# Seven block products for every second down product in a Fourier mixing and SoLU kernel

## The chip, the core and the metric

The kernel runs on one core of a Trainium2 chip, in FP32. The metric is the device time of one execution in microseconds, the median of several runs. The core has TensorE (PE in the profile; its weight loads are PEld), VectorE (DVE), ScalarE (ACT), GpSimd (POOL) and SyncE (SP, which here only issues transfers). Each works through its own instructions in the order of the program, and semaphores make one wait for another.

## The reference, cut to what matters

```python
def _attn_ref(x):                        # x: 8 x 3136 x 256
    X = np.fft.fft(x, axis=1)
    X = np.fft.fft(X, axis=2)
    return X.real.astype(np.float32)

def _moe_ref(x, w_in, w_out, g_ln):      # 25088 x 256, 256 x 1024, 1024 x 256
    h = x @ w_in
    h_max = np.max(h, axis=-1, keepdims=True)
    e = np.exp(h - h_max)
    sm = e / (np.sum(e, axis=-1, keepdims=True) + 1e-09)
    solu = h * sm
    mu = np.mean(solu, axis=-1, keepdims=True)
    var = np.mean((solu - mu) ** 2, axis=-1, keepdims=True)
    ln = (solu - mu) / np.sqrt(var + 1e-06) * g_ln
    return ln @ w_out
```

The output of the first function, as 25088 rows, is the input of the second.

## The kernel before

The Fourier transform over the 3136 positions is split as 49 x 64. The part over 49 is the "first transform" of a pair of batches, the part over 64 the "second transform"; the transform over the 256 features is folded into `w_in`. `g_ln` and the mean are folded into `w_out` (`Wo`), so that what is left after the down product is one scale for each row, `rs`.

A **unit** is one index of the 49-part of one pair of batches: 128 rows of an even part `q[:, 0:128]` and an odd part `q[:, 128:256]`. Even plus and minus odd give two sets of 128 rows, its two *signs*; a unit with index 0 has one sign only. There are 4 pairs of 25 units, 100 in all. Units run as a pipeline of **steps**: step i brings in unit i and does the down product of unit i - 4. Of each unit:

```python
    def up(t, c):                                   # half c of the up product, on TensorE
        ps = ps_h.tile([P, FF], FP32, tag=f"h{c}", name=f"ps_h{c}")
        for half in range(2):
            fs = slice(half * HW, (half + 1) * HW)
            nc.tensor.matmul(ps[:, fs], t.q[:, c * P : (c + 1) * P], Wi[:, c, fs], start=True, stop=True)
        return ps

    # even(t, ps): VectorE, t.ev = w_mid * t.r + ps
    # transform1(pr, s): first transform of a later pair: TensorE into ps_m, ScalarE copies it to z
    # transform2(pr, k1): second transform: TensorE into ps_m; take2(t, ps): ScalarE copies it to t.q
    # spread(t): a small transfer of one row of t.q to t.r

    def join(t, ps):                                # VectorE
        t.nmax = small.tile([P, 2], FP32, tag="nmax", name="nmax")
        for s in t.signs:
            t.h[s] = fpool.tile([P, FF], FP32, tag="h", name="h", bufs=2)
            nc.vector.tensor_tensor_reduce(out=t.h[s], in0=t.h[0] if s else t.ev, in1=ps, ...)

    def expo(t):                                    # ScalarE
        ...
        for s in t.signs:
            nc.scalar.mul(out=t.neg[:, s : s + 1], in_=t.nmax[:, s : s + 1], mul=-1.0)
            t.u[s] = fpool.tile([P, FF], FP32, tag="u", name="u", bufs=2)
            nc.scalar.activation(out=t.u[s], in_=t.h[s], func=ACT.Exp, bias=t.neg[:, s : s + 1],
                                 accum_out=t.esum[:, s : s + 1])

    # product(t, s): VectorE, u = h * u with its sum;  square(t, s): ScalarE, sum of (usum - FF * u)^2

    def stats(t):                                   # GpSimd
        nc.gpsimd.tensor_scalar(out=es[:, n], in0=t.esum[:, n], scalar1=1e-9, scalar2=1e-3, ...)
        nc.gpsimd.tensor_tensor(out=es2[:, n], in0=es[:, n], in1=es[:, n], op=ALU.mult)
        nc.gpsimd.tensor_scalar(out=v[:, n], in0=t.ssq[:, n], scalar1=float(FF) ** -3, ...)
        nc.gpsimd.tensor_tensor(out=v[:, n], in0=v[:, n], in1=es2[:, n], op=ALU.add)
        nc.gpsimd.tensor_tensor(out=t.rs[:, n], in0=v[:, n], in1=neg_half[:, n], op=ALU.pow)

    def turn_blocks(t, s):                          # VectorE: transposes u in 32 x 32 blocks, to v
        ...
    def move_blocks(batch, units, ...):             # 16 transfers put the blocks of two units into uT
        ...
    def down(t, s):                                 # TensorE
        uT = t.batch.uT[:, t.w].rearrange("p c i (n s) -> p c (i n) s", s=2)
        ps = ps_m.tile([P, D], FP32, tag="m", name="ps_o")
        for c in range(KF):                         # KF = 8
            nc.tensor.matmul(ps, uT[:, c, :, s], Wo[:, c, :], start=(c == 0), stop=(c == KF - 1))
        return ps

    # scale(t, s, ps): ScalarE, ot = ps * rs;  store(t): transfers of ot to the output
```

[...] `ps_h0` and `ps_h1` take two each, `ps_m` takes four in turn (`bufs=4`). A step is, cut to the steady part:

```python
            store(units[i - lag - 1])
            begin(i)                     # even(cur, up(cur, 0)); cur.odd = up(cur, 1);
                                         # then transform2, take2 and spread of unit i + 2
            join(cur, cur.odd)
            expo(cur)
            ahead_pe(ahd, cur.k1)        # first transform of the next pair, in some steps
            ps_o = [down(old, s) for s in order]
            for s in cur.signs:
                product(cur, s)
            for s in cur.signs:
                square(cur, s)
                turn_blocks(cur, s)
            scale(old, order[0], ps_o[0])
            move_blocks(batches[-1], slice(0, 2))       # every second step
            stats(cur)
            ahead(ahd, cur.k1)           # loads, mirror sums and folds for the next pair
            scale(old, order[1], ps_o[1])
```

The first four units are turned by TensorE (`turn_whole`), before this loop is in its steady state.

## Time and profile before

| | before |
|---|---|
| time, median of 3 runs | 1189.88 us (1187.1 to 1191.42) |
| span of the profiled run | 1189.0 us |
| granted TensorE clock | 1.00 |
| TensorE / weight loads busy | 1152.6 / 874.5 us |
| VectorE / ScalarE / GpSimd busy | 912.3 / 679.9 / 505.9 us |
| first 100 us / 100 to 1145 us / rest: TensorE busy | 67.66 / 1045.00 / 39.95 us |
| moved by transfers | 185.37 MB, mean 156 GB/s |

An engine's busy time is the union of its instructions. A mean is that of one record; records of TensorE overlap, so that what a pass takes of a stream is read from start to start. The idle time of an engine is put down to what ended it. The last chain is followed back from the end of the span: each step goes to what released the instruction, or to the one before it on its engine.

### The profile page before, as it was taken

Reading aid. Unit: us, or ns where it says so; the run is one execution under the profiler, and the core shown is the slowest. Engines: PE = TensorE matmul, PEld = TensorE weight load, DVE = VectorE, ACT = ScalarE, POOL = GpSimd, SP = SyncE. Lnnn points to the kernel's source line nnn. Section 1 sums busy time; section 2 is a strip of 40 time slices with the busy share of each in tenths; the row PEclk is TensorE's granted clock in tenths of the full one; section 3 lists DMA queues with packets and bytes.
Section 4 is the critical chain, followed back from the end, with each engine's and each line's share of the span. In section 5 each row is a group of like instructions: output and inputs, shape, how many; then the busy total and the mean of one; then the engine's idle time right before and its main releaser. Section 6 shows DMA issues by size and latency. Waiting matters only on the chain.

```text
span 1189.0 us, 15738 instructions
## 1 busy us (share of the span) xinstructions
PE 1152.6 (97%) x4720; PEld 874.5 (74%) x4720; DVE 912.3 (77%) x1234; ACT 679.9 (57%) x1404; POOL 505.9 (43%) x766
## 2 busy tenths in 40 slices
PE   2989999999999999999999999999999999999998
PEld 1556777778777777777777777777777777777787
DVE  6879777777768877787778978777786887877780
ACT  3566665656546656565556656565564665655561
POOL 3025556444544444442644554443553333333323
PEclk9999999999999999999999999999999999999999
DMA  9671989958996766655996887775897464554544
GB/s 231 199 188 27 191 187 193 196 138 165 176 168 165 178 168 167 164 137 140 175 176 170 176 170 166 160 165 133 152 187 142 108 154 97 137 122 116 135 104 117
DMA packets 458452, 185.37 MB, mean 156 GB/s; under 512 B 425750, under 2 KB 440350, under 8 KB 458368
## 3 DMA queue, kind: packets, MB, share of 16 engines
q1 hardware_dynamic: 444608, 146.22, 58.3%
q0 software_dynamic: 13760, 38.16, 12.9%
q8 instruction: 38, 0.62, 0.2%
q14 instruction: 46, 0.38, 0.1%
HBM read 44.78 MB, written 38.80 MB: 70 GB/s over the span
## 4 chain that ended last, share of the span: by engine, by line
PE 93%; DMA 3%; DVE 2%; SPq 1%; issue 1%; POOL 1%; ACT 0%; DVEq 0%; ACTq 0%; POOLq 0%
PE ps_o L325 56%; PE ps_h L227 28%; PE ps L171 5%; PE ps L199 4%; DMA raw_in<-in_moe_w_in_dram 2%; PE wps L456 1%; DMA r<-q 1%; SPq L179 1%; DVE h L241 0%; POOL uT L319 0%; DMA out_dram<-ot,idx 0%; DVE y L123 0%; SPq L442 0%; PE ps_t L305 0%; DVE xa L131 0%
## 5 line engine op out<-in xcount | busy, mean ns | idle before, releaser
L325 PE MATMUL ps_o<-Wo,uT 128*128 128x256 f32 x3136 | 693.4, 379 | 1.3 <-ACT uT L310 0.9
L325 PEld LDWEIGHTS ps_o<-Wo,uT 128*128 128x128 f32 x3136 | 610.8, 196 | 64.0 <-ACT uT L310 1.1
L227 PE MATMUL ps_h<-Wi,q 128*128 128x512 f32 x800 | 360.5, 593 | 5.1 <-DVE ev L233 3.0
L272 POOL TENSOR_SCALAR es<-esum 128x2 f32<-128x2 f32 (+1 forms) x100 | 116.4, 1164 | 425.3 <-ACT u L251 425.1
L258 DVE SCALAR_TENSOR_TENSOR u<-h,u 128x1024 f32<-128x1024 f32 x196 | 239.9, 1225 | 33.5 <-ACT u L251 20.7
L227 PEld LDWEIGHTS ps_h<-Wi,q 128*128 128x128 f32 x800 | 151.5, 190 | 154.3 <-issue 142.3
L265 ACT ACTIVATE h<-u,usum 128x1024 f32<-128x1024 f32 x196 | 224.5, 1147 | 14.8 <-DVE u L258 9.0
L233 DVE SCALAR_TENSOR_TENSOR ev<-w_mid,r,ps_h 128x1024 f32<-128x1024 f32 x100 | 127.8, 1278 | 135.0 <-PE ps_h L227 127.1
L251 ACT ACTIVATE u<-h,neg 128x1024 f32<-128x1024 f32 x196 | 225.6, 1151 | 6.4
L293 DVE STREAM_TRANSPOSE v<-u 128x1024 f32<-128x1024 f32 x192 | 227.5, 1224 | 0.1
L205 ACT COPY q<-ps 128x256 f32<-128x256 f32 x100 | 37.1, 372 | 306.7 <-PE ps L199 279.5
L241 DVE CUSTOM_DVE_ANT_0 h<-ev,ps_h 128x1024 f32<-128x1024 f32 x100 | 122.1, 1221 | 48.9 <-PE ps_h L227 45.3
L330 ACT ACTIVATE ot<-ps_o,rs 128x256 f32<-128x256 f32 x196 | 90.6, 465 | 75.3 <-PE ps_o L325 66.3
L241 DVE CUSTOM_DVE_ANT_0 h<-h,ps_h 128x1024 f32<-128x1024 f32 x96 | 117.3, 1222 | 14.2 <-ACT neg L249 0.5
L337 POOL DMA_INDIRECT out_dram<-ot,idx x96 | 103.1, 1074 | 41.9 <-issue 21.4
L171 PE MATMUL ps<-y,F 98*100 98x258 f32 (+3 forms) x288 | 72.5, 389 | 25.2 <-DVE y L124 25.2
L199 PEld LDWEIGHTS ps<-T,g 128*128 128x128 f32 x400 | 60.2, 191 | 47.4 <-issue 46.9
L249 ACT ACTIVATE neg<-nmax 128x1 f32<-128x1 f32 x196 | 38.8, 198 | 71.0 <-DVE nmax L241 70.9
L280 POOL TENSOR_TENSOR rs<-v,neg_half 128x2 f32<-128x2 f32 (+1 forms) x100 | 71.7, 717 | 7.8
L171 PEld LDWEIGHTS ps<-y,F 98*100 98x100 f32 x288 | 46.3, 179 | 37.6 <-DVE y L124 24.3
L277 POOL TENSOR_SCALAR v<-ssq 128x2 f32<-128x2 f32 (+1 forms) x100 | 22.9, 229 | 117.7 <-ACT h L265 117.6
L199 PE MATMUL ps<-T,g 128*128 128x128 f32 x400 | 60.6, 274 | 0.0
(72 smaller groups left out, 493.9 us busy)
## 6 DMA issues: line engine op xcount, KB each, us to landing
uT<-v SPq DMA_DIRECT2D x752, 128.0 KB
out_dram<-ot SPq DMA_DIRECT2D x100, 128.0 KB
g<-zd POOLq DMA_DIRECT2D x72, 160.0 KB, 5.5
xa<-in_x_dram SPq DMA_DIRECT2D x28, 392.0 KB
zd<-z SPq DMA_DIRECT2D x24, 400.0 KB
raw_in<-in_moe_w_in_dram SPq DMA_DIRECT2D x4, 512.0 KB
raw_out<-in_moe_w_out_dram SPq DMA_DIRECT2D x2, 1024.0 KB
r<-q SPq DMA_DIRECT2D x100, 0.5 KB
```

The costliest lines, as they stand in the source:

```text
L171: nc.tensor.matmul(o[..., cs], F[:, 2 * t + h, :], i[..., cs], start=first, stop=True, skip_group_check=True)
L199: nc.tensor.matmul(o, g[:, k, h * P : (h + 1) * P], table, start=(h == 0), stop=True, skip_group_check=True)
L227: nc.tensor.matmul(ps[:, fs], t.q[:, c * P : (c + 1) * P], Wi[:, c, fs], start=True, stop=True)
L233: nc.vector.scalar_tensor_tensor(out=t.ev, in0=w_mid, scalar=t.r, in1=ps, op0=ALU.mult, op1=ALU.add)
L241: nc.vector.tensor_tensor_reduce(out=t.h[s], in0=t.h[0] if s else t.ev, in1=ps, scale=1.0 if s else -0.5, scalar=-3.0e38, op0=ALU.add, op1 ...
L251: nc.scalar.activation(out=t.u[s], in_=t.h[s], func=ACT.Exp, bias=t.neg[:, s : s + 1], accum_out=t.esum[:, s : s + 1])
L258: nc.vector.scalar_tensor_tensor(out=t.u[s], in0=t.h[s], scalar=1.0, in1=t.u[s], op0=ALU.mult, op1=ALU.mult, accum_out=t.usum[:, s : s + 1])
L265: nc.scalar.activation(out=t.h[s], in_=t.u[s], func=ACT.Square, bias=t.usum[:, s : s + 1], scale=-float(FF), accum_out=t.ssq[:, s : s + 1])
L272: nc.gpsimd.tensor_scalar(out=es[:, n], in0=t.esum[:, n], scalar1=1e-9, scalar2=1e-3, op0=ALU.add, op1=ALU.mult)
L293: nc.vector.transpose(out=t.batch.v[:, t.w, :, o], in_=t.u[s])
L325: nc.tensor.matmul(ps, uT[:, c, :, s], Wo[:, c, :], start=(c == 0), stop=(c == KF - 1))
L337: dma = nc.gpsimd.indirect_dma_start(out=out, out_offset=bass.IndirectOffsetOnAxis(ap=idx[:, i : i + 1], axis=0), in_=t.ot[s], in_offset=None)
```

## The change

A down product of a unit with two signs is a product of 256 rows (two signs of 128) by 1024 by 256. Cut each operand into 2 x 2 blocks: rows by sign (A1x, A2x), the inner 1024 into two halves of four chunks, the 256 columns into two of 128. The plain way needs eight block products. Strassen's scheme (in Winograd's form) needs seven, of sums of blocks. The change does this for every second unit, to take one eighth of the down product off TensorE there. The sums of weight blocks are made once (`Ws`). The sums of blocks of u (`S`, and one in place in A21) are made for each such unit on GpSimd, one step before their use. The seven products share three PSUM banks, by accumulating on top of copies, and spread over two steps: six in one, P4 in the next. To free GpSimd for the sums, the variance goes to ScalarE; only the power stays.

```diff
-    gpool = ctx.enter_context(tc.tile_pool(name="gpool", bufs=6))
+    gpool = ctx.enter_context(tc.tile_pool(name="gpool", bufs=3))
...
-    ps_m = ctx.enter_context(tc.tile_pool(name="ps_m", bufs=4, space=PSUM))
+    spool = ctx.enter_context(tc.tile_pool(name="spool", bufs=2))
+    ps_m = ctx.enter_context(tc.tile_pool(name="ps_m", bufs=1, space=PSUM))
...
+    def result(i):
+        return ps_m.tile([P, 2 * D], FP32, tag=f"m{i % 4}", name="ps_m")
...                                      (both transforms of the steady part now use result(0))
-        es = small.tile([P, 2], FP32, tag="es", name="es")
-        nc.gpsimd.tensor_scalar(out=es[:, n], in0=t.esum[:, n], scalar1=1e-9, scalar2=1e-3, ...)
...                                      (and the next three GpSimd operations)
+        nc.scalar.activation(out=es2[:, n], in_=t.esum[:, n], func=ACT.Square, bias=limits[:, 3:4], scale=1e-3)
+        for s in t.signs:
+            nc.scalar.activation(out=v[:, s : s + 1], in_=t.ssq[:, s : s + 1], func=ACT.Identity, bias=es2[:, s : s + 1],
+                                 scale=float(FF) ** -3)
...
+    def sums(t):
+        A11, A12, A21, A22 = blocks(t)
+        t.S = spool.tile([P, 3, KF // 2, P], FP32, tag="S", name="S")
+        for o, a, b, op in ((t.S[:, 0], A21, A22, ALU.add), (t.S[:, 1], t.S[:, 0], A11, ALU.subtract),
+                            (A21, A11, A21, ALU.subtract), (t.S[:, 2], A12, t.S[:, 1], ALU.subtract)):
+            nc.gpsimd.tensor_tensor(out=o, in0=a, in1=b, op=op)
+
+    def product7(o, a, b, start=False):
+        n = KF // 2
+        for c in range(n):
+            nc.tensor.matmul(o, a[:, c], b[:, c], start=start and c == 0, stop=c == n - 1, skip_group_check=True)
...
+            banks.extend(result(j) for j in (2, 3, 1))
...
+            self.C11, self.C21, self.P53 = (bank(i)[:, 0:P] for i in range(3))
...
+        def p1(self):
+            product7(self.C11, self.A11, Wo[:, 0 : KF // 2, 0:P], True)
+            nc.scalar.copy(self.C21, self.C11)
+        def p5(self):
+            product7(self.P53, self.t.S[:, 0], Ws[:, 0], True)
+            nc.scalar.copy(self.E5, self.P53)
+        def p6(self):
+            product7(self.C21, self.t.S[:, 1], Ws[:, 1])
+            nc.scalar.copy(self.X, self.C21)
+        def p2(self):
+            product7(self.C11, self.A12, Wo[:, KF // 2 :, 0:P])
+            self.scale(0, 0, self.C11)
+        def p7_p3(self):
+            product7(self.C21, self.S3, Ws[:, 2])
+            product7(self.P53, self.t.S[:, 2], Wo[:, KF // 2 :, P:])
+        def sum22(self):
+            nc.vector.tensor_tensor(out=self.C22, in0=self.C21, in1=self.E5, op=ALU.add)
+        def sum12(self):
+            nc.vector.tensor_tensor(out=self.C12, in0=self.P53, in1=self.X, op=ALU.add)
+        def p4(self):
+            product7(self.C21, self.A22, Ws[:, 3])
+            self.scale(0, 1, self.C12)
+            self.scale(1, 1, self.C22)
+            self.scale(1, 0, self.C21)
...
     def down(t, s):
-        ps = ps_m.tile([P, D], FP32, tag="m", name="ps_o")
+        ps = bank(2 * s)[:, 0:D]
```

The loop is written anew from step 5 on. `by_seven(i)` holds for odd units with two signs, but for the last unit. In an odd step `seven` is set, in an even step it is not:

```python
            for s in prv.signs:                  # the unit of the step before
                square(prv, s)
            stats(prv)
            if by_seven(i - lag + 1):
                sums(units[i - lag + 1])
            ps = up(cur, 0)
            if half:
                half.p4(); half = None
            for t, s, ps_o in rest:
                scale(t, s, ps_o)
            rest = []
            if seven:
                half = Down(old, ...); half.p1()
            else:
                ps_o = down(old, order[0])
            other_pairs(i, ahead_pe)             # first transform, in some steps
            even(cur, ps)
            if seven:
                half.p5()
            store(units[i - lag - 1])
            cur.odd = up(cur, 1)
            join(cur, 0)
            if seven:
                half.p6()
            elif len(order) == 2:
                rest.append((old, order[1], down(old, order[1])))
            expo(cur, 0)
            if seven:
                half.p2()
            else:
                scale(old, order[0], ps_o)
            second_transform(i + 2)              # transform2, take2, spread
            join(cur, 1)
            expo(cur, 1)
            if seven:
                half.p7_p3()
            product(cur, 0)
            if seven:
                half.sum22()
            product(cur, 1)
            if seven:
                half.sum12()
            for s in cur.signs:
                turn_blocks(cur, s)
            if cur.w:
                move_blocks(batches[-1], slice(0, 2))
            ...                                  # transfers of the transforms
            other_pairs(i, ahead)
```

(In this listing the tests for the ends of the loop are cut.) The opening puts some of its work areas into `Ws` and `spool`, and `gpool` loads (`turn`) are issued at five chosen steps of a pair.

## The prediction

> **What bounds the kernel now.** I read the page from the top: busy shares, the chain that ended last, the costliest groups, and then the timeline of one steady step. First the busy line of the page, and its chain by engine and by line:

> ```profile
> PE 1152.6 (97%) x4720; PEld 874.5 (74%) x4720; DVE 912.3 (77%) x1234; ACT 679.9 (57%) x1404; POOL 505.9 (43%) x766
> PE 93%; DMA 3%; DVE 2%; SPq 1%; issue 1%; POOL 1%; ACT 0%; DVEq 0%; ACTq 0%; POOLq 0%
> ```

> TensorE is busy 97% of the span and is 93% of the chain. No other engine holds it up in the steady part. The groups that the change touches:

> ```profile
> L325 PE MATMUL ps_o<-Wo,uT 128*128 128x256 f32 x3136 | 693.4, 379 | 1.3 <-ACT uT L310 0.9
> L325 PEld LDWEIGHTS ps_o<-Wo,uT 128*128 128x128 f32 x3136 | 610.8, 196 | 64.0 <-ACT uT L310 1.1
> L272 POOL TENSOR_SCALAR es<-esum 128x2 f32<-128x2 f32 (+1 forms) x100 | 116.4, 1164 | 425.3 <-ACT u L251 425.1
> L330 ACT ACTIVATE ot<-ps_o,rs 128x256 f32<-128x256 f32 x196 | 90.6, 465 | 75.3 <-PE ps_o L325 66.3
> ```

> The down product (L325) is the largest group, 693 us. It has 3136 records for 196 products of eight chunks, so each FP32 matmul is two passes. A mean duration is no price here, since passes overlap. Prices come from start to start, in the timeline of one step (start, duration, engine, line):

> ```profile
> 1006.71 3.60 PE L227 MATMUL ps_h<-Wi,q 128*128 128x512 f32 x8
> ...
> 1010.15 0.61 PE L199 MATMUL ps<-T,g 128*128 128x128 f32 x4
> 1010.15 0.41 PEld L199 LDWEIGHTS ps<-T,g 128*128 128x128 f32 x3 [0.24 <-issue]
> 1010.44 1.22 DVE L241 CUSTOM_DVE_ANT_0 h<-ev,ps_h 128x1024 f32<-128x1024 f32 x1 [0.53 <-PE ps_h L227]
> ...
> 1010.59 7.08 PE L325 MATMUL ps_o<-Wo,uT 128*128 128x256 f32 x32
> 1010.79 0.37 ACT L205 COPY q<-ps 128x256 f32<-128x256 f32 x1 [3.40 <-PE ps L199]
> ...
> 1013.09 0.19 ACT L249 ACTIVATE neg<-nmax 128x1 f32<-128x1 f32 x1
> ...
> 1014.59 1.23 DVE L258 SCALAR_TENSOR_TENSOR u<-h,u 128x1024 f32<-128x1024 f32 x1
> 1014.65 1.21 POOL L272 TENSOR_SCALAR es<-esum 128x2 f32<-128x2 f32 x1 [5.33 <-ACT u L251]
> ...
> 1015.86 1.15 ACT L265 ACTIVATE h<-u,usum 128x1024 f32<-128x1024 f32 x1
> ...
> 1017.00 0.45 ACT L330 ACTIVATE ot<-ps_o,rs 128x256 f32<-128x256 f32 x1
> ...
> 1017.51 1.02 PE L227 MATMUL ps_h<-Wi,q 128*128 128x512 f32 x2
> ```

> Eight up passes take 1010.15 - 1006.71 = 3.44 us (1.72 for each of the two halves), four passes of the second transform 0.44 us, 32 down passes 6.92 us (0.216 each). A step is 10.80 us, all TensorE. In steps that also do part of the next pair's first transform, four more passes come in:

> ```profile
> 701.07 1.03 PE L171 MATMUL ps<-y,F 98*100 98x258 f32 x4
> 701.93 7.07 PE L325 MATMUL ps_o<-Wo,uT 128*128 128x256 f32 x32
> ```

> They add 0.86 us. Two plain steps are 21.6 us, two with the transform 23.3.

> [...] Here the four 128-column passes, each with its own load, come every 0.110 us, half of the 0.216 of 256 columns; the three loads in 0.41 us keep that pace too. [...] ScalarE runs both squares (1014.49 and 1015.86) before the scale at 1017.00, as in the program. [...] in the kernel before they cost almost nothing (0.5 us in total of TensorE waiting for scales). [...] the two-column es operation takes 1.21 us (median; 0.19 at the least), beginning and ending with the VectorE product at 1014.59.

> **The change part by part.** *Block products.* Seven products of four chunks, two passes each, are 56 passes of 128 columns: 56 x 0.110 = 6.16 us in place of 6.92. That removes 0.75 us from a unit, 47 units: 35 us, if TensorE never waits.

> *GpSimd.* It loses four small operations a unit (about 1.8 us, mostly lock wait) and gains four sums of 512 elements every second step; from the GpSimd row of xa<-xa,xb (2341 ns for 1020 elements) I estimate 1.17 us each, 4.7 together. They are issued a step before their use and lie beside other work.

> *VectorE* gains two 128-column sums, [...] every second step. It would need some 20 us of two steps: below TensorE.

> *ScalarE* gains three copies of 128 columns, four quarter scales for two whole ones (0.3 us each, estimated between the 0.20 of 128x1 and the 0.37 of 128x256), and three tiny operations for the variance (0.23 us each by the row of neg and its gap). It stays near 16 us of two steps. So no engine's total becomes the bound. What counts is the order.

> *The order.* Call U the moment when the second up half of an even step ends on TensorE. The code then puts the whole second-sign down product (16 passes, 3.46 us) ahead of the second transform, and ScalarE's copy of that transform (take2) ahead of the second exponential. After that ScalarE does both squares, the variance, and only then the scale of that down product (list `rest`). This scale frees the bank that the product P5 of the odd step overwrites. Along this chain, in us after U: transform data at 3.46 + 0.44 + 0.20 = 4.10 (0.20: 1010.59 to 1010.79); take2 ends 4.47; the second product starts 1.50 after the neg (1013.09 to 1014.59): 6.0; its square 1.27 later (to 1015.86): 7.27; the variance at +1.14: 8.4; three operations: 9.1; the scale ends at 9.56; P5 starts about 9.75. TensorE has only up (1.72), P1 (0.88) and perhaps a transform (0.86) to do after 3.9: it arrives at 6.5, or 7.4. It waits about 3.2 us, or 2.3. Then P5 (0.88) and the second up half (1.72): T = U + 12.35.

> From T to the next U I find no wait: P6, P2, transform, P7, P3, up, P4, down, up are 0.88 + 0.88 + 0.44 + 1.76 + 1.72 + 0.88 + 3.46 + 1.72 = 11.7 us, plus 0.86. P4 needs sum22, which VectorE has at about T + 4.7, and TensorE arrives at T + 5.7.

> So two steps take 12.35 + 11.7 = 24.1 us in place of 21.6 (+2.5), or 24.9 in place of 23.3 (+1.6). There are 45 such pairs of steps (48 odd steps from 5 to 99, less two whose finished unit has one sign, less the first), about half with transforms: 23 x 2.5 + 22 x 1.6 = 93 us. The opening and the drain I take as unchanged within 3 us. 1189.9 + 93 = 1283; with a little for locks and wake-ups, **1285 us**.

> **The rivals.** *The saving arrives.* If the scale of `rest` is in fact not late, TensorE stays the bound and 35 us come off: about 1155 us. For it: 97% busy TensorE and idle shares elsewhere. Against it: queues in program order and one bank for both products. *Weight loads become the bound.* At 0.19 us a load (record length) in series, 56 loads are 10.9 us for 6.9: +4 us a unit, about 1375 us. Against it: three loads in 0.41 us. The loads of L325 read every second element and their records are 196 ns for 190, so a spacing of 0.115 instead of 0.110 is possible; that would be 13 us in all. *GpSimd's sums hold VectorE back* (lock of up to 1.2 us on a product in the chain): +1 us in a pair, 1285 becomes 1330 at worst. *Late transfers.* P4 keeps the transposed buffer a step longer, so the 16 block moves start later. In this trace a move takes some 0.9 us of its queue; 16 are 14 us, done some 4 us ahead of need in a 24 us period. Hidden, I think.

> **Range and chances.** The chain is made of measured pieces, but has ten hand-overs; 0.1 us on each pair's whole is 4.5 us. A missed release or overlap could halve the wait (about 1235); locks could bring 1310. I take 1225 to 1315 for eight in ten. The chance that the chain does not hold at all and the saving shows is 0.10 for over 2% faster; 0.08 for within 2%; 0.82 for slower.

> **What would show it.** In the profile after: TensorE idle some 110 to 150 us more, in 45 waits of two to three us, put down to ScalarE's ot scale (or what stands ahead of it) just before the P5 passes; its busy share near 87% (1152.6 - 35 of 1285). Passes of the seven products 0.110 us apart. Two steps of 24 to 25 us in the timeline. VectorE and ScalarE shares below 80% and 65%. Wrong would be: TensorE still at 97% and pairs of steps near 20.8 us (the first rival), spacing near 0.19 (the second), waits of TensorE for sums or moves (the others).

## The result and the profile after

The changed kernel takes 1403.5 us (median of 4 runs, 1397.4 to 1407.5) against 1190.0 us: ratio 1.1793, 95% interval 1.1744 to 1.1842. The direction was predicted, the size was not: 213 us instead of 95, far outside the range.

The page of the kernel after, first the busy line, the granted TensorE clock by slices, the chain by engine, then two groups:

```profile
PE 1230.4 (88%) x5850; PEld 934.1 (67%) x5850; DVE 971.3 (69%) x1329; ACT 788.2 (56%) x1935; POOL 586.5 (42%) x558
...
PEclk9999999999899999989999999999989999899898
...
issue 45%; POOL 23%; PE 11%; DMA 6%; SPq 5%; DVE 4%; ACT 4%; POOLq 0%; DVEq 0%; ACTq 0%
...
L238 PE MATMUL ps_h<-Wi,q 128*128 128x512 f32 x800 | 421.2, 654 | 1.9 <-DVE nmax L252 1.6
...
L268 DVE SCALAR_TENSOR_TENSOR u<-h,u 128x1024 f32<-128x1024 f32 x196 | 267.8, 1368 | 93.0 <-ACT u L261 92.7
```

TensorE's share fell to 88%, but its busy time rose by 78 us although passes were taken away. The up product, which the change doesn't touch, has a mean of 654 ns where it had 593, and VectorE's product 1368 where it had 1225 (the same two groups on the page of the kernel before):

```profile
L227 PE MATMUL ps_h<-Wi,q 128*128 128x512 f32 x800 | 360.5, 593 | 5.1 <-DVE ev L233 3.0
L258 DVE SCALAR_TENSOR_TENSOR u<-h,u 128x1024 f32<-128x1024 f32 x196 | 239.9, 1225 | 33.5 <-ACT u L251 20.7
```

The mean granted clock is 0.933 where it was 1.000. So there are waits, and work beside them that became slower. The view of waits has, of TensorE's own:

```profile
PE ps_m L355 <- ACT ot L426: 94.5, 35, 5.5
...
PE ps_m L182 <- DVE y L128: 28.1, 9, 3.4
```

The first is the predicted wait: block products (L355) for ScalarE's scale of the second-sign down product (L426), 35 times where 45 were predicted. The second, of the first transform for a fold on VectorE, was not predicted. One plain pair of steps in the timeline (start, duration, engine, line):

```profile
1164.62 0.61 PE L210 MATMUL ps_m<-T,g 128*128 128x128 f32 x4
...
1166.78 1.10 PE L355 MATMUL ps_m<-Wo,uT 128*128 128x128 f32 x8
...
1170.16 0.45 ACT L426 ACTIVATE ot<-ps_m,rs 128x256 f32<-128x256 f32 x1
...
1170.76 2.05 PE L355 MATMUL ps_m<-Ws,S 128*128 128x128 f32 x8 [2.88 <-ACT ot L426]
...
1172.60 3.62 PE L238 MATMUL ps_h<-Wi,q 128*128 128x512 f32 x4
...
1176.01 1.43 PE L355 MATMUL ps_m<-Ws,S 128*128 128x128 f32 x8
```

P5 starts 0.15 us after the scale ended. Eight passes that took 0.89 us elsewhere take 1.84 (to 1172.60), and four up passes 3.41 instead of 1.72. The stretches of the same pair (us, busy time of each engine and count, then granted clock, DMA share, GB/s) say why:

```profile
1166.78:1170.76 3.98, 1.10 (x10) 0.94 (x8) 3.71 (x5) 3.78 (x11) 0.41 (x1) 0.90 0.84 177
1170.76:1172.60 1.84, 1.84 (x9) 1.84 (x9) 0.97 (x1) 0.02 (x1) 1.34 (x2) 0.50 0.68 155
1172.60:1176.01 3.41, 3.41 (x5) 1.35 (x5) 0.00 (x0) 0.27 (x1) 0.00 (x0) 0.50 0.48 136
1176.01:1177.28 1.27, 1.27 (x10) 1.27 (x8) 0.93 (x1) 0.00 (x0) 0.00 (x0) 0.69 0.00 0
1177.28:1191.79 14.51, 14.51 (x79) 11.96 (x78) 10.69 (x18) 9.16 (x23) 7.18 (x7) 1.00 0.27 60
```

After the wait TensorE is granted half its clock for 5.25 us; the 0.69 of the next stretch is a mean over the change back to full. That is 0.95 + 1.69 + 0.38 = 3.0 us lost on top of the 2.9 waited. The pair takes 1191.79 - 1164.62 = 27.2 us. Not every pair loses so much. Of the 19 waits of 2.88 us, 9 have 6.83 us of half clock at their end, as this one (from 1169.96 on), and their pairs take 27.1 to 27.2 us; ten have 3.41 us, and a plain pair takes 25.6 to 25.9.

### The profile page after: what moved, and what is told of

It is laid out like the page before. It is cut to its first block, busy times and chain, and to the rows that moved or that the text cites. A ratio compares the mean times of both kernels' runs of the same rounds, so it can differ in the third digit from the quotient of the medians.

```text
span 1402.7 us, 18541 instructions
## 1 busy us (share of the span) xinstructions
PE 1230.4 (88%) x5850; PEld 934.1 (67%) x5850; DVE 971.3 (69%) x1329; ACT 788.2 (56%) x1935; POOL 586.5 (42%) x558
## 4 chain that ended last, share of the span: by engine, by line
issue 45%; POOL 23%; PE 11%; DMA 6%; SPq 5%; DVE 4%; ACT 4%; POOLq 0%; DVEq 0%; ACTq 0%
POOL S L350 9%; SPq L326 5%; POOL out_dram L433 5%; PE ps_h L238 4%; PE ps_m L355 3%; POOL xa L137 3%; PE ps_m L421 3%; DMA uT<-v 3%; POOL rs L287 2%; POOL g L198 2%; DMA room<-in_x_dram 2%; ACT h L275 2%; DVE h L252 1%; POOL xb L117 1%; DVE u L268 1%
## 5 line engine op out<-in xcount | busy, mean ns | idle before, releaser
L238 PE MATMUL ps_h<-Wi,q 128*128 128x512 f32 x800 | 421.2, 654 | 1.9 <-DVE nmax L252 1.6
L421 PE MATMUL ps_m<-Wo,uT 128*128 128x256 f32 x1632 | 371.0, 381 | 5.1 <-ACT ot L426 2.9
L421 PEld LDWEIGHTS ps_m<-Wo,uT 128*128 128x128 f32 x1632 | 317.1, 197 | 59.2 <-issue 23.0
L268 DVE SCALAR_TENSOR_TENSOR u<-h,u 128x1024 f32<-128x1024 f32 x196 | 267.8, 1368 | 93.0 <-ACT u L261 92.7
L261 ACT ACTIVATE u<-h,neg 128x1024 f32<-128x1024 f32 x196 | 225.3, 1150 | 6.4
L355 PEld LDWEIGHTS ps_m<-Ws,S 128*128 128x128 f32 x752 | 129.4, 249 | 143.8 <-issue 137.4
L355 PE MATMUL ps_m<-Ws,S 128*128 128x128 f32 x752 | 134.0, 336 | 98.7 <-ACT ot L426 93.4
L182 PE MATMUL ps_m<-y,F 98*100 98x258 f32 (+3 forms) x288 | 83.2, 421 | 58.5 <-DVE y L128 28.1
L355 PEld LDWEIGHTS ps_m<-Wo,uT 128*128 128x128 f32 x752 | 100.4, 198 | 22.8 <-issue 20.5
L355 PEld LDWEIGHTS ps_m<-Ws,uT 128*128 128x128 f32 x752 | 99.8, 197 | 22.2 <-issue 20.8
L355 PE MATMUL ps_m<-Wo,uT 128*128 128x128 f32 x752 | 104.5, 282 | 1.1 <-ACT ot L426 1.1
L355 PE MATMUL ps_m<-Ws,uT 128*128 128x128 f32 x752 | 103.8, 281 | 0.7 <-DVE E L402 0.7
L182 PEld LDWEIGHTS ps_m<-y,F 98*100 98x100 f32 x288 | 48.0, 188 | 80.9 <-ACT ps_m L383 28.5
```

Of the source, the lines that this page charges most:

```text
L182: nc.tensor.matmul(o[..., cs], F[:, 2 * t + h, :], i[..., cs], start=first, stop=True, skip_group_check=True)
L268: nc.vector.scalar_tensor_tensor(out=t.u[s], in0=t.h[s], scalar=1.0, in1=t.u[s], op0=ALU.mult, op1=ALU.mult, accum_out=t.usum[:, s : s + 1])
L355: nc.tensor.matmul(o, a[:, c], b[:, c], start=start and c == 0, stop=c == n - 1, skip_group_check=True)
```

## The experiments

Theory A: the wait for the scale, and the half clock that follows it, make the loss. Its rivals: B, the block products are slow in themselves; C, the new loop, the buffers or the variance on ScalarE; D, a second wait, for the fold; E, GpSimd's sums shut VectorE out; F, which came up on the way, the new order of a step as such, the place of the second up half above all. Ratios are to the kernel before.

**1. The wait filled with thrown-away work** (fill).

```diff
             if seven:
+                ps = ps_h.tile([P, FF], FP32, tag="h1", name="ps_fill")
+                for half_f in (0, 1, 0):
+                    ... one half of up(cur, 1) into ps
                 half.p5()
```

> The changed kernel, with three half up products (2.58 us of passes into a bank that is free then, results thrown away) put on TensorE just before P5 in each odd step: more work, in the place where TensorE waits for the scale. Theory A (the wait of 2.9 us lets the granted clock fall to a half, and P5, the second up half and P6 then take 3 us more): the clock stays at 1.0, two plain steps take 24.2 us in place of 27.2, the whole 1290 to 1330 us. Theory B (those products are slow for a reason of their own, the block operands or GpSimd's sums): no pair of steps becomes shorter, the whole 1400 us or more.

1375.0 us, ratio 1.156 [1.154, 1.159]; clock 0.986. TensorE's timeline:

```profile
1038.67 2.74 PE L814 MATMUL ps_fill<-Wi,q 128*128 128x512 f32 x6
1041.72 1.13 PE L355 MATMUL ps_m<-Ws,S 128*128 128x128 f32 x8 [0.30 <-ACT ot L426]
1042.68 1.88 PE L238 MATMUL ps_h<-Wi,q 128*128 128x512 f32 x4
```

With 2.6 us more work in it, the plain pair is shorter: from this 1038.67 to the next at 1062.90 it is 24.2 us, not 25.6 to 27.2, and P5 and the up half have their full speed. That is theory A's pair to a tenth, and the predicted pair (24.1) too. The total missed its 1290 to 1330: in pairs with a transform TensorE waits earlier, for the fold, and there the added work only adds (they take up to 30.8 us). So D was open.

**2. Only the scale moved ahead of the squares** (scale_first), **and both moved behind P1's copy** (late_squares).

```diff
+            for t, s, ps_o in rest:
+                scale(t, s, ps_o)
+            rest = []
             if prv:
                 for s in prv.signs:
                     square(prv, s)
                 stats(prv)
```

(scale_first, the same three lines taken out below; late_squares has the squares and `stats` after `half.p1()` instead)

> The changed kernel with one move in the order of ScalarE: the scale of the even step's second down product comes before the two squares and the variance, not after them. Theory A: TensorE's wait ahead of P5 goes, a wait of about 0.6 us ahead of P6 (its copy is still behind the squares) takes its place, two plain steps take 21.5 us, the clock stays above 0.98, the whole 1185 to 1225 us. Theory B (the block products themselves are what costs): 1350 us or more.

> The changed kernel with the squares and the variance moved behind the scale and behind the copy after P1, so that neither P5 nor P6 waits for them. Theory A: a wait of about 0.7 us ahead of P4 is left (sum22 on VectorE, which now runs later); two plain steps take 21.3 to 21.8 us, the whole 1170 to 1210 us. Theory B: 1350 us or more.

1277.0 us, 1.0745 [1.0727, 1.0763], and 1282.9 us, 1.080 [1.077, 1.083]. Three moved lines are worth 126 us. Plain pairs came to 21.5 us, as A said, but the totals missed their ranges by 50 us and more. Pairs with a transform still took 23.9 to 29.6 us, with waits like this (scale_first, TensorE):

```profile
501.70 2.00 PE L182 MATMUL ps_m<-y,F 98*100 98x258 f32 x4 [3.40 <-DVE y L128]
503.49 1.91 PE L355 MATMUL ps_m<-Ws,S 128*128 128x128 f32 x8
505.19 3.34 PE L238 MATMUL ps_h<-Wi,q 128*128 128x512 f32 x4
```

The first transform waits 3.40 us for the fold of the step before, and half clock follows again (0.86 us of passes take 1.79).

**3. No seven products in the new loop** (plain).

```diff
         def by_seven(i):
-            return i % 2 and i < len(units) - 1 and len(units[i].signs) == 2
+            return False
```

> The changed kernel with no unit by seven products: the new loop, the variance on ScalarE, fewer buffers, and the old down product for every unit; all values are the reference's. Theory A (only the wait ahead of P5 and what follows from it costs): TensorE's passes cover the chain (10.8 us a step), 1188 to 1210 us. Theory C (the new order, the single bank of the two transforms or the variance on ScalarE cost most of the loss): 1280 us or more.

1235.0 us, 1.038 [1.036, 1.040]. One thing differs from what was written: the first sums, which overwrite a block of unit 1, were left in, so that unit's output isn't the reference's. Steady steps are 10.8 us. C is a quarter of the loss at most, but 46 us is more than the 20 expected. Experiments 4 and 8 bear on the rest.

**4. The first transform one step later**, alone and with the scale's move (later_transform, scale_later).

```diff
-                if step == START[pr.p == 1][c] + 2 + half:
+                if step == START[pr.p == 1][c] + 3 + half:
```

> The changed kernel with the first transform of the later pairs one step later, so that it no longer waits for a fold that VectorE has only just begun. Theory D (a second new wait, of TensorE for the fold, 3.4 us in steps 30 to 44 of the run without P5's wait, costs beside P5's wait): those pairs of steps go from 29.1 to about 27 us, steps without a transform stay at 27.2, the whole 1360 to 1390 us. Theory A alone (P5's wait is all): no change, 1395 to 1410 us.

> Both moves: the scale ahead of the squares, and the first transform one step later. Theory A with D: pairs with transforms come to 22.5 to 23.5 us, plain pairs stay at 21.5, the whole 1195 to 1225 us. If the two waits aren't what the pairs with transforms lose (GpSimd's lock, late transfers), they stay at 24 to 28 us, the whole 1250 to 1280 us.

1381.2 us, 1.162 [1.160, 1.164], and 1233.6 us, 1.036 [1.034, 1.039]. D is real: 22 us while P5's wait stands, 43 us once it is gone. In the first case P5's wait fills part of the gap (its total rises from 94.5 to 114.7 us). scale_later was still 9 us over its range.

**5. Sums left out** (no_sums): GpSimd makes them for the first unit alone, and all units use these; the output isn't the reference's.

```diff
+        if t.k1 > 1 or t.p:
+            t.S = units[1].S
+            return
```

> The changed kernel without the sums of blocks on GpSimd (made for the first such unit alone and used again for all; the block in place is left as it is): the output isn't the reference's. Theory E (GpSimd's sums shut VectorE's products and folds out, which draws out the chain): VectorE's product comes back from 1368 ns to 1230 and the fold from 1334 to 680, the whole 1375 to 1395 us. If the sums cost nothing, 1400 us; if they are the main cost, under 1300 us.

1356.1 us, 1.140 [1.138, 1.142]. VectorE's product comes back to its old duration:

```profile
L268 DVE SCALAR_TENSOR_TENSOR u<-h,u 128x1024 f32<-128x1024 f32 x196 | 241.7, 1234 | 112.3 <-ACT u L261 112.1
```

One of the fold's two operations (L129) does too, first in the changed kernel, then in no_sums:

```profile
L129 DVE TENSOR_TENSOR y<-xa 98x508 f32<-98x508 f32 x28 | 37.4, 1334 | 0.0
L129 DVE TENSOR_TENSOR y<-xa 98x508 f32<-98x508 f32 x28 | 19.0, 678 | 0.0
```

What the prediction and the expectations call a lock shows in the kernel before: 93 of GpSimd's 100 es operations (L272) start at most 0.07 us after a VectorE product, end 0.05 us after its end and take 1.21 us; the three with no product beside them take 0.19 us.

E holds, with 47 us where 8 to 28 were expected: a delayed product stands in the chain to P5 and lengthens the wait (a product of 3.26 us went with a wait of 4.05 us). The sums act on the product by a detour. Of 19 products over 1.4 us in the changed kernel (1.59 to 3.36 us, where the median is 1.23), 16 stand beside GpSimd's mirror sum, which the kernel before has too, and three beside a sum of blocks; in no_sums the mean, 1234 ns, is within 9 ns of the kernel before's. So it is mostly the shift in GpSimd's queue that puts the mirror sum on the product. The fold is drawn out beside the sums of blocks themselves (14 of 28 take 1.98 to 2.00 us there, the other 14 0.68). By the mean clocks of the two profiled runs (94.0 and 71.0 us not granted), 23 of the 38 us between them are the clock's. But E is not the main cause, though the page's chain gave GpSimd 23% and "issue" 45%.

**6. The variance back on GpSimd** (gpsimd_variance; the four old operations in place of the three of ScalarE).

> The changed kernel with the variance back on GpSimd, as before the change (that part undone alone). Theory A: three operations leave the chain on ScalarE, 0.76 us by the trace, so P5's wait falls from 2.88 to about 2.1 us; waits of 2.0 us were not followed by a half clock in the trace, so most of the 3 us after them may go too: plain pairs 23.4 to 24 us, the whole 1310 to 1360 us, the clock above 0.95. If the variance on ScalarE is not in the chain: 1395 us or more.

1341.8 us, 1.129 [1.127, 1.131]; clock 0.971. TensorE:

```profile
1242.04 1.13 PE L358 MATMUL ps_m<-Ws,S 128*128 128x128 f32 x8 [2.18 <-ACT ot L429]
...
1265.56 1.13 PE L358 MATMUL ps_m<-Ws,S 128*128 128x128 f32 x8 [2.18 <-ACT ot L429]
1266.53 1.88 PE L238 MATMUL ps_h<-Wi,q 128*128 128x512 f32 x4
```

0.70 us less in the chain brings the wait from 2.88 to 2.18 us, the full clock mostly stays (half clock comes with four of 19 such waits), and most plain pairs take 1265.56 - 1242.04 = 23.5 us in place of 25.6 to 27.2: 2.1 to 3.7 us for 0.7. What was written of waits of 2.0 us is wrong: in the changed kernel half clock came with five of eight.

**7. Three orders meant to be better** (reordered, p4_later, one_step). reordered: late_squares, the later transform, and in even steps the second transform ahead of the second down product. p4_later: P4 behind the first down product. one_step: P4 in the step of the other six. The last two also do the last such unit the plain way.

> A version that is meant to be better than both: squares and variance behind the copy after P1 (so behind the scale), first transform one step later, and in even steps the second transform ahead of the second down product, so that the second exponential doesn't wait for it. Theory A with D: plain pairs 21.0 to 21.4 us, with transforms 22.3 to 23, the whole 1170 to 1200 us. If late transfers of the transposed blocks hold it, waits of 3 us ahead of a down product and 1210 us or more.

> The reordered version with P4 of an even step behind the first down product (VectorE's sum22 is then surely there) and the last seven-product unit, whose sums came late in the drain, done the plain way. Theory A with D: the waits ahead of P4 (9.8 us in all) and the 3.5 us in the drain go, plain pairs stay at 21.2, the whole 1200 to 1215 us. If the block moves, which P4 now lets start later, are what holds it: more waits for transfers and 1220 us or more.

> The reordered version with all seven products in one step: VectorE's sum22 before its first product, P4 right behind P3, its scales at the start of the next step; the last seven-product unit the plain way. The transposed buffer is no longer held into the next step. If P4's place (waits for sum22, 9.8 us, and moves that start late) is what still holds the reordered version: 1195 to 1210 us. If the moves are late because VectorE's transposes end late, P4's place does nothing for them: 1210 to 1225 us.

1222.1 us, 1.029 [1.027, 1.032]; 1242.4 us, 1.042 [1.038, 1.046]; 1212.2 us, 1.022 [1.018, 1.027]. reordered and p4_later were above the range of A with D, and p4_later went up; one_step lies in the range written for moves that are late because VectorE's transposes end late. SyncE's waits in p4_later:

```profile
SPq L326 <- DVE v L300: 157.6, 45, 6.5
SPq L326 <- PE ps_m L355: 98.1, 36, 9.0
```

The block moves (L326) wait for VectorE's transposes and here for P4 (98 us, 36 times; in the changed kernel once). TensorE's waits ahead of down products then sum to some 44 us, in place of 14 in reordered. The rival "late transfers" of the prediction is real, but only once the first two waits are gone and P4 stands later still.

**8. The same order without seven products, then the old order of a step** (reordered_plain, old_order, old_order_plain). In the old order both up halves and the second transform come first, as before the change:

```diff
+            begin(i)                       # both up halves, second transform
+            d.p1(); d.p5()                 # or down(old, first sign)
+            join(cur, 0); expo(cur, 0)
+            d.copy5(); d.p6()
+            join(cur, 1); expo(cur, 1)
+            other_pairs(i, ahead_pe)
+            d.p2(); d.p7_p3()              # or down(old, second sign)
+            product(cur, 0); square(cur, 0)
+            d.sum22(); d.p4()
+            product(cur, 1); square(cur, 1)
+            d.sum12(); turn_blocks; d.scales4(); move_blocks; stats; ahead
```

> The reordered version with no unit by seven products and no sums: every down product the old way, all else as in the reordered version (variance on ScalarE, fewer buffers, one bank for the transforms). It parts what the order brings from what the products bring. If the seven products gain on balance once TensorE needn't wait for them: 1235 us or more. If their 0.4 us a pair (21.2 for 21.6) is less than the waits for sums, locks and block moves that they bring: 1190 to 1210 us.

> Seven products in the old order of a step: both up halves and the second transform first, then the down products, squares in the step of their unit, P4 in the same step as the rest, P1's copy ahead of the exponentials, the other copies between them. Theory F (the rest of the loss, 2%, comes from the second up half standing behind a down product: joins, transposes and block moves of each unit end 3 to 5 us later in the step): no wait ahead of P5, odd steps 10.35 us, even steps 10.8, the whole 1170 to 1190 us, so faster than both. If the seven products bring their own waits (sums, locks): 1200 us or more.

> The same old order of a step with no unit by seven products: what is left of the change is the variance on ScalarE, the fewer buffers and the one bank of the transforms. Theory F: 1187 to 1195 us, the kernel before's. If buffers, bank or variance are what costs 2%: 1205 to 1220 us.

1215.1 us, 1.022 [1.020, 1.024]; 1188.6 us, 0.9992 [0.9982, 1.0001]; 1193.2 us, 1.0033 [1.0020, 1.0045]. reordered_plain lies in neither of its ranges: in the new order the seven products lose 7 us (1222.1 against 1215.1). F holds for the order as a whole: with no block product in either, the order of the step parts 1215 from 1193. The old order also puts the squares back into the step of their unit and moves both transforms, so that the place of the up half alone is not shown to be the cause. Fewer buffers, the one bank and the variance on ScalarE are worth 0.3% together. In the old order seven products are no loss, but gain only 5 us of the 22 that 47 odd steps of 10.33 in place of 10.79 us should give.

**9. The last two waits taken away; seven products in every unit** (no_late_ends, every_unit).

```diff
-            return i % 2 and i < len(units) - 1 and len(units[i].signs) == 2
+            return i % 2 and i < len(units) - 4 and len(units[i].signs) == 2
-    START = [..., [4, 6, 8, 10, 12, 13, 15, 16]]
+    START = [..., [3, 5, 7, 9, 11, 13, 15, 17]]
```

(every_unit: `0 < i < len(units) - 4` in place of the first condition)

> The old-order version with seven products, without its two kinds of waits that are left: the last seven-product unit, whose sums came 5.6 us late in the drain, is done the plain way, and the first transforms of the second pair are spread so that no step has two of them in the one bank (4.5 us of waits). Each wait was followed by passes at half clock. If these are what parts 1188.6 us from 1193 - 45 x 0.46 = 1172: 1170 to 1180 us, faster than both. If not: 1185 us or more.

> The same with seven products in every unit with two signs, not in every second. If TensorE stays the bound: steps of 10.33 us, another 20 us off, 1150 to 1160 us. If GpSimd's sums (5.1 us a unit) and their lock make VectorE, which was at 84%, the bound: 1180 us or more, with waits of TensorE for VectorE.

no_late_ends: 1175.1 us, 0.9886 [0.9871, 0.9901], faster than both kernels. Its busy line, then two steps:

```profile
PE 1134.9 (97%) x5826; PEld 883.4 (75%) x5826; DVE 1006.9 (86%) x1327; ACT 785.5 (67%) x1930; POOL 644.0 (55%) x554
```

```profile
1067.97 3.60 PE L238 MATMUL ps_h<-Wi,q 128*128 128x512 f32 x8
...
1078.30 3.60 PE L238 MATMUL ps_h<-Wi,q 128*128 128x512 f32 x8
...
1089.09 1.45 PE L238 MATMUL ps_h<-Wi,q 128*128 128x512 f32 x3
```

TensorE is at 97% again, the odd step takes 10.33 us, the even one 10.79. Both edits together, against the two waits of old_order (5.6 us in the drain for the sums, 4.5 us for the bank of the transforms), brought 13.5 us.

every_unit: 1213.6 us, 1.022 [1.020, 1.023]. GpSimd rises to 76% and its sums wait and draw out:

```profile
L350 POOL TENSOR_TENSOR S<-S,uT 128x512 f32<-128x512 f32 x92 | 173.7, 1888 | 7.3
L350 POOL TENSOR_TENSOR S<-uT 128x512 f32<-128x512 f32 x92 | 147.4, 1602 | 96.3 <-DMA out_dram<-ot 45.1 <-DMA r<-q 24.9 <-DMA uT<-v 11.0
```

VectorE's product takes 1767 ns on average. So GpSimd carries the sums of every second unit and not those of every one; nothing between was run.

## Why the prediction was wrong in size

- **The bound and the chain: right.** P5 was put 9.75 us after U; in the trace U is 1161.17 (the second down product's start), and P5 starts at 1170.76, 9.59 later. The wait was put at 3.2 us and is 2.88. It is at the place and behind the operation named.
- **The step that failed:** "Then P5 (0.88) and the second up half (1.72): T = U + 12.35." These two terms, and P6's 0.88 after them, were priced at full clock. They took 1.84, 3.41 and 1.27 us, most of it at half clock: a pair of 27.2 us in place of 24.1. fill, with the clock kept up, gave 24.2. The mean clock of 0.933 over 1402.7 us is 94 us of full-clock passes not granted (part of it in the waits themselves). The prediction holds no term for the clock. In the trace of the changed kernel it falls to 0.50 in 41 places, 25 times for 3.41 us and 15 times for 6.83 (the last, of 2.61 us, lies at the trace's end), each of these 40 behind 1.87 us or more of idle TensorE within 3.41 us (last section).
- **The idle time "some 110 to 150 us more": right, in part by luck.** It rose from 36.4 to 172.3 us, by 136. Busy time was to fall by 35 us and rose by 78, and that is nearly the whole miss. The predicted wait makes 94.5 us of the idle time; the waits for the fold, below, are in it too.
- **"From T to the next U I find no wait ... plus 0.86": wrong in steps with a transform.** In the kernel before, VectorE's transposes ended just before TensorE's step did (at 696.94 and 697.19 us in one of them); in the changed one they end in the next step, 5.5 us after its start (507.63 and 502.12), and the fold comes behind them, while the transform stands early in the step. That wait (3.4 us, half clock with it) is worth 22 to 43 us.
- **The sums "lie beside other work": half wrong.** They take 1.50, 1.29, 1.04 and 1.30 us by their medians, 5.1 together, near the estimate of 4.7. With the clock behind the longer waits they cost 47 us in place of "a little".
- **The saving of 0.75 us a unit:** passes with S as weights come every 0.112 us (0.89 for eight), those with blocks of u, which lie at every second element, every 0.117 (0.94). 4 x 0.94 + 3 x 0.89 = 6.43 in place of 6.16: 0.46 to 0.49 saved. The second rival named this size.
- **"Late transfers hidden, I think": right for the changed kernel**, and wrong for each version without its waits, up to the old order.
- **Opening and drain within 3 us:** right for the opening (the first up product of step 5 starts at 99.4 us, before at 100.2), wrong for the drain: from the last up product to the end 44.3 us in place of 38.8, with a wait of 4.2 us for the sums in it.

Of the 213 us, taken away one after the other: 126 with the scale's move, 43 with the later transform, 21 with the orders up to one_step, 24 with the old order of a step, 13 with the two ends; in all 228, and so 15 us below the kernel before. Not settled: which part of the order of a step makes the 24 us, how E's share that is not the clock's divides, and which of fewer buffers, bank and variance makes the last 0.3%.

## What to carry to other kernels

When TensorE is the bound and a saving on it is planned, follow the release of each bank that it writes next through the queue of the engine that gives it. Here the release stood behind two squares and the variance of a younger unit, and moving it ahead of them was worth 126 us. Then ask how a TensorE wait falls on the clock: here each of the 37 full-clock windows of 3.41 us with 2.00 us or more of idle TensorE was followed by 3.41 or 6.83 us at half clock, and a wait of 2.9 us cost 1.4 to 3.0 us more behind it. Look at the granted clock by stretches, not at its mean. Where the order of a step is rebuilt for a trick, run the new order without the trick: here the order lost what the trick won, and the trick in the old order gained 1.1%.

## What the runs showed of the hardware

The traces of the two kernels record the granted clock as 1.00 or 0.50, and each of its changes (81 in the changed kernel, one in the kernel before) lies at a multiple of 3.41 us from its first record. Cut into these windows, the changed kernel shows how waits of one length differ (TensorE's busy time, then granted clock, DMA share, GB/s; three windows, each with the next one):

```profile
832.04:835.45 3.41, 1.68 (x11) 1.00 0.72 156
835.45:838.87 3.42, 3.13 (x17) 1.00 0.83 202
...
859.35:862.76 3.41, 1.40 (x10) 1.00 0.85 161
862.76:866.17 3.41, 3.41 (x8) 0.50 0.82 265
...
1166.55:1169.96 3.41, 1.33 (x9) 1.00 0.87 184
1169.96:1173.37 3.41, 2.61 (x9) 0.50 0.70 152
```

The page's chain, right in the kernel before, pointed at GpSimd and "issue" after the change, 68% together; taking GpSimd's sums out brought 47 of 213 us. A view of TensorE's own waits, and the timeline of one pair, found the cause.
